# S4 plus eight experts on one core: S4 totals in one bf16 pass, weights' totals by DRAM, first block's transposed x kept, second block's operands stored in parts

## The chip, the core and the metric

The kernel runs on one core of a Trainium2 chip. The metric is the device time of the whole program in microseconds (us), lower is better. Times given are those of separate runs; the profile is of one further execution.

## The reference, cut to what matters

```python
xn = layernorm(u)                                   # 2048 tokens x 512
# S4: a convolution over the tokens, one kernel K for each of 512 channels
P = exp(logdA[:, :, None] * l); K = einsum("dn,dnl,dn->dl", Cc, P, dB).real
y = irfft(rfft(pad(xn.T)) * rfft(pad(K)))[:, :2048].T + xn * Dskip
# eight experts, all of them taken by every token (K = 8 of E = 8)
gates = softmax(xn @ w_gate)                        # sorted, then matched to e
for e in range(8):
    out += gates[:, e] * (silu(xn @ w1[e]) @ w2[e])   # w1 512x1792, w2 1792x512
return u + y + out
```

Inputs and results are float32.

## The kernel before

**Numbers in two halves.** TensorE works in float16. Every operand is split into a high and a low float16 half (`a = hi + lo`), and a product is three matmuls: hi·hi, hi·lo, lo·hi. So that the halves don't leave the range of float16, each operand is first scaled by a power of two that is worked out on the chip. For that a tile is squared with its row sums, the 128 row sums are added over the partitions, and the exponent of that *total* gives the scale. The addition over partitions is `pow2_total`: a float32 matmul with `ones` (128x128, float32) as weights and the row sums as a moving column; the result, in every partition, is copied out of PSUM by ACT. The tile is `tot_<name>`: `tot_k...` for the S4 kernels (32 of them), `tot_w...` for the experts' weights (two per expert, the first expert's w1 apart, 15 in all), `tot_a` and `tot_b` at the start.

**The experts.** Tokens are taken in NB = 4 blocks of 512, the hidden width 1792 in 7 pairs of 2x128, grouped as quads `d` = (0,1), (2,3), (4,5), (6). For each expert e, each block tb and each quad d, `block` makes the products of w1 in a Strassen-like form: seven products of combined operands (`xop`, seven combinations `o` of the four quarters of x, each in two halves `b`; `w1s`, seven combinations of w1), added in three PSUM tiles `hb` and partly in DRAM-accumulated SBUF tiles (`scC`, `scB` receive `sE` by an accumulating DMA of POOL's queue, L1493 `add`). ACT takes Silu from `hb` or `scC`/`scB` (L1324), writes the high half `ahl` (L1328), DVE the low half (L1337). `pop` then issues the second product with w2 (L1291 to L1293) into `y`, and `evacuate` scales it by the gate into `ye` (L1266) and adds it to `oacc` in DRAM through POOL (L1269). The products `product` (L1308) are matmuls of 128x256, the y matmuls 128x512. Expert 0's block 0 (`plain`, L1575) has no combined operands: it uses the transposed x of the first stage, `xT0`, and multiplies plainly.

**Slots.** The kernel is one long program with an order written out by hand. Each quad has four slots, each block sixteen; a slot is some 4.6 us of TensorE work. In `slot` the order is: functions of `mid`, then second products, low halves, functions of `side`, one or two steps of `work_on`, and then `bg_run`, the S4 work. `at(n, f)` puts f into slot n of expert 0; `early` and `copied` stand at other places of a slot. Every engine takes its queue in that order, so an instruction that waits holds up all behind it on its engine.

**Combined x.** For blocks 1 to 3 of expert 0, and again for block 0 (its combined operands are needed from expert 1 on), a stage in halves `(g, a)` works: `x_sums` (DVE), `x_high` (ACT), `x_low` (DVE), four `x_turn` (28 transposes in two matrices, L274, into the bank `s4`; ACT copies them into `xs`, L285, and SP stores them in `xd[g]`). Block 1's go straight to `xop`, and after the last one `xop` is stored whole in `xd[1]`: one DMA of 1.75 MB (L282). At each block's last quad `xop[:, o]` is loaded for the next block in seven parts.

**Weights.** While expert e−1 runs, the weights of expert e are read twice: `pp` tiles for the squares (`piece_square`), then `piece_end` (row sum, total, scales: three Items, each at least two slots after the other and only where the bank `s4` is free), then `raw` tiles for the split (`w1_split`, `w2_split`), which may begin once the third step is done.

**S4.** It is a generator whose DVE cost is paced: `bg_run` lets it run until its DVE estimate has used up `SHARE` × the TensorE time that has passed. Its matmuls (transforms `kf` L800, `uf` L787, `yp` L860, the kernels `kgen` L729, the totals) share one PSUM bank, tag "s4": `take_bank` gives it to a new user after the last one has been read, `bank_free` issues the pending read and says whether a new user may come. S4's result lands in `ys4`; in the last block `s4_final(i)` adds it to `oacc[i]` (POOL, L1477) and stores the output, one call at slot ⌊3i/4⌋. The last block's four tiles are loaded again by `final_load` and finished by DVE.

**SP's queue** carries all other loads and stores.

The lines that set the pace and the places of the moved work:

```python
own = SHARE * (clock["pe"] - clock["pe0"])
...
halves = [(g, a) for g in (2, 3, 0) for a in range(2)]
...
put((E - 1, NB - 1, i * 3 // 16, i * 3 // 4 % 4), lambda i=i: s4_final(i))
```

Of the kernel before, what the change touches and what calls it, by code (L numbers as in the profile page):

```python
# [8 lines left out]

F32 = mybir.dt.float32  # L10
F16 = mybir.dt.float16
I32 = mybir.dt.int32
AF = mybir.ActivationFunctionType
ALU = mybir.AluOpType
# [18 lines left out]
def s4_moe_kernel(  # L33
# [40 lines left out]

    ident = cp.tile([P, P], F16, name="ident")
    make_identity(nc, ident)
    ones = cp.tile([P, P], F32, name="ones")
    V.memset(ones, 1.0)
    halfpi = cp.tile([P, 1], F32, name="halfpi")
    V.memset(halfpi, math.pi / 2)  # L80
# [10 lines left out]
    oacc = [dr.tile([P, D], F32, name=f"oacc{i}") for i in range(NT)]  # L91
    ys4 = dr.tile([P, NT, D], F32, name="ys4")
    xnd = dr.tile([P, NT, D], F32, name="xnd")
    kds = [dr.tile([P, 4, 64], F32, name=f"kd{n}") for n in range(2)]


    uts = {}

    clock = {"slot": 0, "pe": 0.0, "pe0": 0.0, "dve": 0.0, "dve0": 0.0, "left": 0.0,
             "act": 0.0, "act0": 0.0, "pe1": 0.0, "actleft": 0.0}  # L100
    bank = {"out": None, "at": -1}

    def take_bank(out=None):
# [6 lines left out]

    def bank_free():

        if bank["out"]:
            take_bank()
        return clock["slot"] > bank["at"]

# [43 lines left out]

    def pow2_total(rows, n, nm, out=None):

        st = sb.tile([P, n], F32, tag="p2a", name=f"st_{nm}", bufs=2)
        def read():
            S.copy(st, tot[:, :n])
            if out:
                out()
        take_bank(read)
        tot = ps_s.tile([P, 512], F32, tag="s4", name=f"tot_{nm}")
        T.matmul(tot[:, :n], ones, rows, start=True, stop=True)  # L170
        return st

    def pow2_scale(dst, st, nm, add=0):
# [43 lines left out]
    xs_ = {}  # L217

    def x_stats(g):
        if g:  # L220
            xs_["rs8", g] = norm_stats(g)
        else:
            rs8 = xs_["rs8", 0] = sb.tile([P, TPB], F32, tag="rs8", name="rs8again")
            V.tensor_scalar(rs8, rstd[:, 0:TPB], float(2 ** XSH), None, op0=ALU.mult)

    def x_sums(g, a):

# [32 lines left out]
    def x_turn(g, a, q):  # L260


        hi, lo = xs_["hi"], xs_["lo"]
        if g == 1:
            parts = [(r // 4, r // 2 % 2, r % 2) for r in range(8 * q, min(8 * q + 8, 28))]
        else:
            b, o0 = q // 2, q % 2 * 4
            no = min(4, 7 - o0)
            parts = [(o0 + r // 2, b, r % 2) for r in range(2 * no)]
        n = len(parts)  # L270
        take_bank()
        tp = ps_s.tile([P, 8, P], F16, tag="s4", name=f"tp{g}_{a}_{q}")
        for r, (o, b, k) in enumerate(parts):
            T.transpose(tp[:, r, :], (hi, lo)[b][:, o, k * P:(k + 1) * P], ident)  # L274
        if g == 1:
            dst = xop.rearrange("p o a k t -> p (o a k) t")[:, 8 * q:8 * q + n, a * P:(a + 1) * P]
            if q % 2:
                V.tensor_copy(dst, tp[:, :n, :])
            else:
                S.copy(dst, tp[:, :n, :])  # L280
            if a and q == 3:
                nc.sync.dma_start(xd[1], xop)  # L282
        else:
            xs = sb.tile([P, 4, 2, P], F16, tag="hh", name=f"xs{g}_{a}_{q}", bufs=9)
            S.copy(xs.rearrange("p o k t -> p (o k) t")[:, :n], tp[:, :n, :])  # L285
            clock["act"] += at_(n * P)
            bank["at"] = now()
            for k in range(2):
                nc.sync.dma_start(xd[g][:, o0:o0 + no, b, k, a * P:(a + 1) * P], xs[:, :no, k])

    xp = {}

    def xplain(j, rs8):

        xn = sb.tile([P, D], F32, tag="fa", name=f"xn{j}")
# [161 lines left out]

    def w1_split(e, pr, raw):

        dst = w1s[pr].rearrange("p a o c -> p a (o c)")  # L460
        return hilo(dst[:, :, 0:6 * P], raw[:, 0:3, :].rearrange("p o c -> p (o c)"), w1_scale(e, pr))

# [2 lines left out]
        return hilo(dst[:, :, 6 * P:14 * P], tw.rearrange("p o c -> p (o c)"), w1_scale(e, pr))  # L465

    def w2_split(e, pr, raw):
        return hilo(w2s[pr].rearrange("p a f d -> p a (f d)"), raw.rearrange("p a c -> p (a c)"), scales[e][:, 1:2])

    class Item:  # L470
# [26 lines left out]
        return it  # L497

    def piece_end(e, w, n, ready):
        st = {}  # L500

        def s0(raw):
            st["g"] = prepass_end(e, w, n)
            step(0)
            clock["dve"] += 0.2

        def step(n):
            st["at"] = now()
            next(st["g"], None)
            done.add((e, w, n))  # L510

        def s1(raw):
            step(1)

        def s2(raw):
            step(2)
            clock["dve"] += 2.5
# [4 lines left out]
        for it in its:  # L522
            it.e, it.w = e, w
        return its

    def fetch():

# [344 lines left out]
    def at_(n):  # L872

        return n / 1050 + 0.17
# [10 lines left out]
    def now():  # L885
        return clock["slot"]
# [196 lines left out]
    def first_square(w, n, t, on_dve):  # L1083
# [2 lines left out]
        junk = tf  # L1086
        if w == 0:
            junk = w1s[n % 5 + 2][:, n // 5 % 2, 0:tf.shape[1] // TH, :].rearrange("p o c -> p (o c)")
            junk = junk.bitcast(mybir.dt.bfloat16)
# [93 lines left out]
    def plan(e):  # L1183
# [5 lines left out]
                work.append(piece_square(e, w, pr, at(1 + w)))  # L1189
            work.extend(piece_end(e, w, NPR, at(1 + w)))  # L1190
        def made(what, d):
            return lambda: (e - 1, NB - 1, what, d) in done and (e, "py".index(what), 2) in done
# [6 lines left out]
        yield from s4_all()  # L1199

    bg = background()
    SHARE = 0.90

    def bg_run():

# [217 lines left out]
    at(16, lambda: load_x(2))  # L1423
    at(42, s4_dft_load)
    at(19, lambda: x_sums(2, 0))
    halves = [(g, a) for g in (2, 3, 0) for a in range(2)]
    for n, (g, a) in enumerate(halves):
        s0 = 20 + 4 * n
        at(s0, lambda g=g, a=a: x_high(g, a), copied if n == 0 else side)
# [8 lines left out]
            turns.add(n1 - 2)  # L1438
        if a == 0:
            at(s0 + 3, lambda g=g: x_sums(g, 1))  # L1440
            if g:
                at(s0 + 3, lambda g=g: load_x((g + 1) % NB))
        elif g:
            if g + 1 < NB:
                at(s0 + 1, lambda g=g: norm_sums(g + 1))
            at(s0 + 2, lambda g=g: x_stats((g + 1) % NB))
            at(s0 + 3, lambda g=g: x_sums((g + 1) % NB, 0))

    def slot(e, tb, d, s, pops):
        for f in mid.get((e, tb, d, s), ()):  # L1450
# [215 lines left out]
```

## Time and profile before

| | |
|---|---|
| three runs | 2342.41, 2340.79, 2341.77 us; median 2341.77 |
| profiled execution | 2342.11 us, span 2340.3 us |
| granted TensorE clock, mean of the span | 0.998 |
| busy of the span | PE 99%, PEld 66%, DVE 84%, ACT 63%, POOL 15% |
| instructions | 45514 |
| DMA | 319.68 MB, mean 137 GB/s; 331079 packets |

PE is the matmul part of TensorE and PEld its weight loads, which overlap the matmuls; the printed lengths of matmuls overlap each other too, so what one costs is read from the distance between two starts. DVE is VectorE, ACT ScalarE, POOL GpSimd, SP the engine that issues most DMAs. A row of groups reads: line, engine, operation, output <- inputs, shape, count | busy us, mean ns of one | idle time just before, and what ended it. A row of the timeline reads: start, length, engine, line, operation, output <- inputs, shape, and in brackets the wait before it and its releaser.

### The profile page before, as it was taken

What the parts mean: (1) busy time and instruction counts of PE and PEld (TensorE: products, weight loads), DVE (VectorE), ACT (ScalarE), POOL (GpSimd) and SP (SyncE); (2) the same over time, 40 slices, a digit from 0 to 9 for tenths busy, and PEclk for the clock granted to TensorE, in tenths of its full rate; (3) what the DMA queues carried; (4) which work ended last, traced back from release to release, by engine and by line L of the source; (5) the groups of instructions that cost most, each with busy time, mean ns of one, the idle gap of its engine ahead of it and who ended that gap; (6) DMA issues with size and microseconds to landing.
All of it is one profiled execution on the core that took longest, in us unless ns stands there. A gap on an engine that the chain in (4) does not pass through costs nothing.

```text
span 2340.3 us, 45514 instructions
## 1 busy us (share of the span) xinstructions
PE 2323.6 (99%) x17818; PEld 1552.0 (66%) x17818; DVE 1965.9 (84%) x3821; ACT 1472.9 (63%) x2593; POOL 340.6 (15%) x394
## 2 busy tenths in 40 slices
PE   8999999999999999999999999999999999999999
PEld 4666666666666666666666666666666666666665
DVE  8864878889898899999999989999899988997721
ACT  7677667556666576665766657666566665764543
POOL 0001001121111211101111101111111110111112
PEclk9999999999999999999999999999999999999999
DMA  7586556674566655644556546565465653643456
GB/s 252 176 240 166 142 143 159 156 154 108 128 154 163 146 115 132 159 118 105 127 122 160 121 101 136 127 149 119 100 147 121 145 128 90 153 89 71 80 116 146
DMA packets 331079, 319.68 MB, mean 137 GB/s; under 512 B 190896, under 2 KB 224176, under 8 KB 330544
## 3 DMA queue, kind: packets, MB, share of 16 engines
q1 hardware_dynamic: 274416, 222.65, 32.6%
q0 software_dynamic: 55872, 93.61, 25.4%
q8 instruction: 139, 2.28, 0.4%
q14 instruction: 76, 0.62, 0.1%
q10 hardware_dynamic: 576, 0.52, 0.1%
HBM read 202.14 MB, written 65.01 MB: 114 GB/s over the span
## 4 chain that ended last, share of the span: by engine, by line
PE 93%; issue 2%; DMA 2%; ACT 2%; DVE 1%; POOL 0%; SPq 0%; DVEq 0%; POOLq 0%; ACTq 0%
PE hb L1308 41%; PE y L1293 15%; PE y L1292 15%; PE y L1291 15%; PE kgen L729 1%; PE kf L800 1%; PE yp L860 1%; PE uf L787 1%; DMA scB<-sE 1%; PE hb L1575 1%; DMA scC<-sE 0%; DMA oacc<-ye 0%; PE tp L274 0%; ACT ahl L1328 0%; ACT fa L1324 0%
## 5 line engine op out<-in xcount | busy, mean ns | idle before, releaser
L1308 PE MATMUL hb<-xop,w1s 128*128 128x256 f16 x9114 | 1072.9, 273 | 2.6 <-ACT scC L1522 2.4
L1308 PEld LDWEIGHTS <-w1s 128*128 128x128 f16 x9114 | 889.0, 98 | 171.2 <-issue 4.7
L1291 PE MATMUL y<-w2s,ahl 128*128 128x512 f16 x1792 | 679.2, 379 | 1.0 <-ACT ye L1266 1.0
L1293 PE MATMUL y<-w2s,ahl 128*128 128x512 f16 x1792 | 679.2, 379 | 0.0
L1292 PE MATMUL y<-w2s,ahl 128*128 128x512 f16 x1792 | 679.2, 379 | 0.0
L1293 PEld LDWEIGHTS <-ahl 128*128 128x128 f16 x1792 | 175.3, 98 | 211.4
L1493 POOL DMA_DIRECT2D scC<-sE x124 | 118.0, 951 | 1292.5 <-ACT sE L1522 1094.0
L1324 ACT ACTIVATE fa<-hb,sc 128x512 f32<-128x512 f32 (+1 forms) x252 | 160.5, 637 | 196.4 <-PE hb L1308 195.9
L1292 PEld LDWEIGHTS <-ahl 128*128 128x128 f16 x1792 | 175.3, 98 | 162.3 <-issue 1.3
L832 DVE TENSOR_TENSOR s<-s,tm 128x720 f32<-128x720 f32 (+14 forms) x480 | 268.9, 560 | 16.6
L1291 PEld LDWEIGHTS <-ahl 128*128 128x128 f16 x1792 | 175.3, 98 | 161.1
L831 DVE TENSOR_TENSOR tm<-v,k 128x720 f32<-128x720 f32 (+14 forms) x480 | 267.6, 557 | 10.3
L1337 DVE SCALAR_TENSOR_TENSOR ahl<-fa,sc,ahl 128x512 f16<-128x512 f32 (+1 forms) x262 | 178.8, 683 | 59.9 <-ACT ahl L1328 59.5
L1537 ACT COPY hb<-hb 128x512 f32<-128x512 f32 x124 | 64.2, 518 | 238.7 <-PE hb L1308 238.6
L1328 ACT ACTIVATE ahl<-fa,sc 128x512 f16<-128x512 f32 (+1 forms) x262 | 175.8, 671 | 8.5
L1527 ACT COPY hb<-hb 128x512 f32<-128x512 f32 x124 | 64.3, 519 | 175.2 <-PE hb L1308 174.3
L1493 POOL DMA_DIRECT2D scB<-sE x124 | 108.0, 871 | 424.1 <-ACT scB L1522 283.1
L1337 DVE SCALAR_TENSOR_TENSOR ahl<-scB,sc,ahl 128x512 f16<-128x512 f32 x124 | 84.5, 681 | 81.9 <-ACT ahl L1328 78.2
L717 DVE TENSOR_TENSOR tb<-ta,tt 128x64 f32<-128x64 f32 (+2 forms) x192 | 132.0, 688 | 5.7
L711 DVE TENSOR_TENSOR ta<-tb,zr 128x64 f32<-128x64 f32 (+2 forms) x192 | 131.7, 686 | 5.4
L1269 POOL DMA_DIRECT2D oacc<-ye x108 | 96.1, 1343 | 252.7 <-ACT ye L1266 251.1
L714 DVE TENSOR_TENSOR tt<-tb,zi 128x64 f32<-128x64 f32 (+2 forms) x192 | 130.5, 680 | 0.0
(245 smaller groups left out, 2444.2 us busy)
## 6 DMA issues: line engine op xcount, KB each, us to landing
xop<-xd SPq DMA_DIRECT2D x210, 256.0 KB, 4.0
pp<-in_w_dram SPq DMA_DIRECT2D x98, 512.0 KB, 4.2
raw<-in_w_dram SPq DMA_DIRECT2D x56, 512.0 KB, 4.7
oacc<-ye POOLq DMA_DIRECT2D x108, 256.0 KB, 6.3
scC<-sE POOLq DMA_DIRECT2D x93, 256.0 KB, 4.4
scB<-sE POOLq DMA_DIRECT2D x93, 256.0 KB, 4.0
raw<-in_w_dram SPq DMA_DIRECT2D x52, 256.0 KB, 3.8
raw<-in_w_dram SPq DMA_DIRECT2D x104, 128.0 KB, 3.7
```

Source lines behind the costliest of these rows:

```text
L711: V.tensor_tensor(ta, tin, zrv, op=ALU.mult)
L717: V.tensor_tensor(tout, ta, tt, op=ALU.add)
L831: V.tensor_tensor(tm, v3f[:, :, 0:n], kb, op=ALU.mult)
L832: V.tensor_tensor(s3[:, :, m:], s3[:, :, m:], tm, op=ALU.add)
L1291: T.matmul(y, lhs[0], w2s[pr][:, 0, fh, :], start=(c == 0), stop=False)
L1292: T.matmul(y, lhs[0], w2s[pr][:, 1, fh, :], start=False, stop=False)
L1293: T.matmul(y, lhs[1], w2s[pr][:, 0, fh, :], start=False, stop=(c == NF - 1))
L1308: T.matmul(dst[:, q, :], w1s[pr][:, a, wo, k * P:(k + 1) * P], xop[:, xo, b, k, :], start=(first_mm and q == 0 and n == 0), stop=(n == 5), ...
L1324: S.activation(fa, src[:, :n], AF.Silu, scale=w1_unscale(e, d if whole else prs[0]))
L1328: S.activation(ahl[:, 0, :n], fa, AF.Copy, scale=scales[e][:, 3:4])
L1337: V.scalar_tensor_tensor(ahl[:, 1, :n], fa, sc[:, 3:4], ahl[:, 0, :n], op0=ALU.mult, op1=ALU.subtract)
L1493: nc.gpsimd.dma_start(dst, src, accum_op=ALU.add)
```

## The change

Four parts, with some smaller ones.

- *Totals in one pass.* `ones` becomes bfloat16, and `pow2_total` reads the row sums as their upper 16 bits (`bitcast` to bfloat16, every second column). The scale depends on the exponent of the total. This holds for the 32 totals of S4, for `tot_a`, `tot_b` and expert 0's w2.
- *Weights' totals by DRAM.* For the experts from 1 on (14 totals) the matmul is replaced: row sum (DVE), `total_send` (SP stores 128 numbers), `total_fetch` (SP loads them into all partitions), an empty step, `total_sum` (ACT copies with a running sum), scales (DVE). `piece_end` is one Item of six steps, each at least two slots after the last. It asks no longer for the bank.
- *First block's x kept.* `xT0` is sent to DRAM (`x0_send`: normalized x in four stores, three of its quarters' pairs straight into `xd[0]` in six, the whole as `x0d`) in slots 2 to 11, loaded again (`x0_load`), and the four other combinations are made from it by DVE and ACT (`x0_sums`, `x0_high`, `x0_low`, slots 35 to 40), already transposed. The stage's halves (0, 0) and (0, 1) with their transposes go.
- *Block 1's operands in parts.* `xd[1]` is stored in seven DMAs of 256 KB, one a slot from slot 20 on, in place of the one after the last `x_turn`.
- *Smaller.* `SHARE` 0.905; the calls of `s4_final` regrouped in the first slots of each half quad; `clock["two"]` keeps the reads of the bank out of the second step of a slot with two steps of weight work; the first stage's `xn` tiles lie in the ring "hh".

```diff
-    ones = cp.tile([P, P], F32, name="ones")
+    ones = cp.tile([P, P], BF16, name="ones")
...
         if bank["out"]:
+            if clock["two"]:
+                return False
             take_bank()
...
+        high = rows.bitcast(BF16)[:, 1::2]
...
-        T.matmul(tot[:, :n], ones, rows, start=True, stop=True)
+        T.matmul(tot[:, :n], ones, high, start=True, stop=True)
...
+    def total_send(row, nm):
+        rd = dr.tile([P, 1], F32, name=f"rd_{nm}")
+        nc.sync.dma_start(rd, row)
+        return rd
+    def total_fetch(rd, nm):
+        bt = sb.tile([P, P], F32, tag="bt", name=f"bt_{nm}", bufs=1)
+        nc.sync.dma_start(bt, rd.rearrange("p a -> (p a)").partition_broadcast(P))
+        return bt
+    def total_sum(bt, nm):
+        st = sb.tile([P, 1], F32, tag="p2a", name=f"st_{nm}", bufs=2)
+        S.activation(bt, bt, AF.Copy, accum_out=st)
+        clock["act"] += at_(P) + 0.2
         return st
...
-            if a and q == 3:
-                nc.sync.dma_start(xd[1], xop)
...
+    def x0_send(n):
+        if n < 4:
+            nc.sync.dma_start(xnd[:, n, :], xp["xn", n])
+        elif n < 7:
+            k, t = ((0, 0), (2, 0), (2, TH))[n - 4]
+            for b in range(2):
+                nc.sync.dma_start(xd[0][:, n - 4, b], xT0[:, b, k:k + 2, t:t + TH])
+        else:
+            nc.sync.dma_start(x0d, xT0)
+    def x0_load():
+        xs_["x0"] = sb.tile([P, 2, KT, TB], F16, tag="tb", name="x0", bufs=1)
+        nc.sync.dma_start(xs_["x0"], x0d)
+    def x0_sums(k):
+        x0 = xs_["x0"]
...
+        V.tensor_tensor(r.rearrange("p h a t -> p h (a t)"), x0[:, 0, k::2, :], x0[:, 1, k::2, :], op=ALU.add)
+        V.tensor_tensor(s, r[:, 0, 1, :], r[:, 1, 1, :], op=ALU.add)
+        V.tensor_tensor(f[:, 0, :], s, r[:, 0, 0, :], op=ALU.subtract)
+        V.tensor_tensor(f[:, 1, :], r[:, 0, 1, :], r[:, 0, 0, :], op=ALU.subtract)
+        V.tensor_tensor(f[:, 2, :], r[:, 1, 0, :], f[:, 0, :], op=ALU.subtract)
+    def x0_high(k):                       # two ACT copies into hi
...
+    def x0_low(k):                        # two DVE subtractions into lo
...
+        for b, x in enumerate((hi, lo)):
+            nc.sync.dma_start(xd[0][:, 3:7, b, k, :], x)
...
-        st = pow2_total(r, 1, f"w{e}_{w}")
-        yield
-        if bank["out"]:
-            take_bank()
+        if e:
+            rd = total_send(r, f"w{e}_{w}")
+            yield
+            bt = total_fetch(rd, f"w{e}_{w}")
+            yield
+            yield
+            st = total_sum(bt, f"w{e}_{w}")
+            yield
+        else:
...
     def piece_end(e, w, n, ready):
...
-        def later():
-            return now() > st["at"] + 1 and bank_free() and now() + 1 not in turns
-        its = [Item(None, [s0], ready), Item(None, [s1], later), Item(None, [s2], later)]
+        it = Item(None, [lambda raw, k=k: step(k) for k in range(6)],
+                  lambda: now() > st["at"] + 1 if "at" in st else ready())
...
+        clock["two"], n2 = False, limit
...
+            clock["two"] = limit == 0 and n2 == 2
...
-    SHARE = 0.90
+    SHARE = 0.905
...
-    halves = [(g, a) for g in (2, 3, 0) for a in range(2)]
+    halves = [(g, a) for g in (2, 3) for a in range(2)]
...
+    for o in range(7):
+        at(20 + o, lambda o=o: nc.sync.dma_start(xd[1][:, o], xop[:, o]))
+    for n in range(4):
+        at(2 + n // 2, lambda n=n: x0_send(n))
+        at(8 + n, lambda n=n: x0_send(4 + n))
+    for k in range(2):
+        at(35 + 3 * k, lambda k=k: x0_sums(k))
+        at(36 + 3 * k, lambda k=k: x0_high(k))
+        at(37 + 3 * k, lambda k=k: x0_low(k))
...
-        put((E - 1, NB - 1, i * 3 // 16, i * 3 // 4 % 4), lambda i=i: s4_final(i))
+        n = (i + 2) // 3
+        put((E - 1, NB - 1, n // 2, n % 2 * 3), lambda i=i: s4_final(i))
```

More of the change, by code (lines that the diff above doesn't have):

```diff
@@ L11 @@
 F16 = mybir.dt.float16
+BF16 = mybir.dt.bfloat16
 I32 = mybir.dt.int32
@@ L93, in s4_moe_kernel @@
     xnd = dr.tile([P, NT, D], F32, name="xnd")
+    x0d = dr.tile([P, 2, KT, TB], F16, name="x0d")
     kds = [dr.tile([P, 4, 64], F32, name=f"kd{n}") for n in range(2)]
@@ L99, in s4_moe_kernel @@
     clock = {"slot": 0, "pe": 0.0, "pe0": 0.0, "dve": 0.0, "dve0": 0.0, "left": 0.0,
-             "act": 0.0, "act0": 0.0, "pe1": 0.0, "actleft": 0.0}
+             "act": 0.0, "act0": 0.0, "pe1": 0.0, "actleft": 0.0, "two": False}
     bank = {"out": None, "at": -1}
@@ L169, in pow2_total @@
         tot = ps_s.tile([P, 512], F32, tag="s4", name=f"tot_{nm}")
-        T.matmul(tot[:, :n], ones, rows, start=True, stop=True)
+        T.matmul(tot[:, :n], ones, high, start=True, stop=True)
+        return st
+    def total_send(row, nm):
[10 more added lines that the diff above has]
+        clock["act"] += at_(P) + 0.2
         return st
@@ L219, in x_stats @@
     def x_stats(g):
[L220 to L224, printed above, removed]
+        xs_["rs8", g] = norm_stats(g)
     def x_sums(g, a):
@@ L289, in x_turn @@
                 nc.sync.dma_start(xd[g][:, o0:o0 + no, b, k, a * P:(a + 1) * P], xs[:, :no, k])
+    def x0_send(n):
[12 more added lines that the diff above has]
+        x0 = xs_["x0"]
+        r = sb.tile([P, 2, 2, TH], F32, tag="k4", name=f"x0r{k}", bufs=1)
+        f = xs_["f0"] = sb.tile([P, 3, TH], F32, tag="v3", name=f"x0f{k}", bufs=1)
+        s = xs_["s0"] = sb.tile([P, TH], F32, tag="z", name=f"x0s{k}", bufs=1)
+        V.tensor_tensor(r.rearrange("p h a t -> p h (a t)"), x0[:, 0, k::2, :], x0[:, 1, k::2, :], op=ALU.add)
[4 more added lines that the diff above has]
+    def x0_high(k):
+        hi = xs_["hi"] = sb.tile([P, 4, TH], F16, tag="ta", name=f"x0h{k}", bufs=1)
+        S.copy(hi[:, 0], xs_["s0"])
+        S.copy(hi[:, 1:4].rearrange("p o t -> p (o t)"), xs_["f0"].rearrange("p o t -> p (o t)"))
+        clock["act"] += at_(4 * TH)
+    def x0_low(k):
+        hi = xs_["hi"]
+        lo = sb.tile([P, 4, TH], F16, tag="tt", name=f"x0l{k}", bufs=1)
+        V.tensor_tensor(lo[:, 0], xs_["s0"], hi[:, 0], op=ALU.subtract)
+        V.tensor_tensor(lo[:, 1:4].rearrange("p o t -> p (o t)"), xs_["f0"].rearrange("p o t -> p (o t)"),
+                        hi[:, 1:4].rearrange("p o t -> p (o t)"), op=ALU.subtract)
+        for b, x in enumerate((hi, lo)):
+            nc.sync.dma_start(xd[0][:, 3:7, b, k, :], x)
     xp = {}
     def xplain(j, rs8):
-        xn = sb.tile([P, D], F32, tag="fa", name=f"xn{j}")
+        xn = xp["xn", j] = sb.tile([P, D], F32, tag="hh", name=f"xn{j}", bufs=9)
         V.tensor_scalar(xn, uts[0][j], mean[:, j:j + 1], rs8[:, j:j + 1], op0=ALU.subtract, op1=ALU.mult)
@@ L407, in prepass_end @@
         yield
-        st = pow2_total(r, 1, f"w{e}_{w}")
-        yield
-        if bank["out"]:
-            take_bank()
+        if e:
[7 more added lines that the diff above has]
+        else:
+            st = pow2_total(r, 1, f"w{e}_{w}")
+            yield
+            if bank["out"]:
+                take_bank()
         if w == 0:
@@ L458, in w1_split @@
     def w1_split(e, pr, raw):
+        assert e == 0 or (e, 0, 5) in done
         dst = w1s[pr].rearrange("p a o c -> p a (o c)")
@@ L467, in w2_split @@
     def w2_split(e, pr, raw):
+        assert e == 0 or (e, 1, 5) in done
         return hilo(w2s[pr].rearrange("p a f d -> p a (f d)"), raw.rearrange("p a c -> p (a c)"), scales[e][:, 1:2])
@@ L499, in piece_end, with step @@
     def piece_end(e, w, n, ready):
[L500 to L507, printed above, removed]
+        st = {"g": prepass_end(e, w, n)}
+        def step(k):
             st["at"] = now()
             next(st["g"], None)
[L510 to L517, printed above, removed]
-        def later():
-            return now() > st["at"] + 1 and bank_free() and now() + 1 not in turns
-        its = [Item(None, [s0], ready), Item(None, [s1], later), Item(None, [s2], later)]
-        for it in its:
-            it.e, it.w = e, w
-        return its
+            done.add((e, w, k))
+            clock["dve"] += (0.2, 0.0, 0.0, 0.0, 0.0, 0.9)[k]
+        it = Item(None, [lambda raw, k=k: step(k) for k in range(6)],
+                  lambda: now() > st["at"] + 1 if "at" in st else ready())
+        it.e, it.w = e, w
+        return [it]
     def fetch():
@@ L1088, in first_square @@
             junk = w1s[n % 5 + 2][:, n // 5 % 2, 0:tf.shape[1] // TH, :].rearrange("p o c -> p (o c)")
-            junk = junk.bitcast(mybir.dt.bfloat16)
+            junk = junk.bitcast(BF16)
         r = rows_of(0, w)[:, n:n + 1]
@@ L1191, in made @@
         def made(what, d):
-            return lambda: (e - 1, NB - 1, what, d) in done and (e, "py".index(what), 2) in done
+            return lambda: (e - 1, NB - 1, what, d) in done and (e, "py".index(what), 5) in done
         a = [piece_w1(e, pr, made("p", d)) for d, prs in enumerate(DQS) for pr in prs]
@@ L1440, in s4_moe_kernel @@
             at(s0 + 3, lambda g=g: x_sums(g, 1))
[L1441 to L1447, printed above, removed]
+            at(s0 + 3, lambda g=g: load_x(g + 1) if g + 1 < NB else x0_load())
+        elif g + 1 < NB:
+            at(s0 + 1, lambda g=g: norm_sums(g + 1))
+            at(s0 + 2, lambda g=g: x_stats(g + 1))
+            at(s0 + 3, lambda g=g: x_sums(g + 1, 0))
+    for o in range(7):
[7 more added lines that the diff above has]
+        at(37 + 3 * k, lambda k=k: x0_low(k))
     def slot(e, tb, d, s, pops):
```

## The prediction

> **What bounds the kernel now.** I read the page's busy line and its chain first, then the waits, then single stretches of the timeline.
>
> ```profile
> PE 2323.6 (99%) x17818; PEld 1552.0 (66%) x17818; DVE 1965.9 (84%) x3821; ACT 1472.9 (63%) x2593; POOL 340.6 (15%) x394
> PE 93%; issue 2%; DMA 2%; ACT 2%; DVE 1%; POOL 0%; SPq 0%; DVEq 0%; POOLq 0%; ACTq 0%
> PE hb L1308 <- ACT scC L1522: 2.4, 4, 0.9
> ```
>
> TensorE is the end-setting engine for 93% of the chain, and its largest listed wait in the whole span is 2.4 us. So a matmul that goes away is worth its issue interval, and little else is to be had. An issue interval is read from the starts in the timeline (the printed lengths overlap):
>
> ```profile
> 328.23 0.28 PE L170 MATMUL tot_k<-krow,ones 128*128 128x1 f32 x2
> 328.37 0.81 PE L1308 MATMUL hb<-xop,w1s 128*128 128x256 f16 x6
> 201.54 0.24 PE L353 MATMUL lg<-wgs,xop 128*128 128x8 f16 x4
> 201.64 2.12 PE L1308 MATMUL hb<-xop,w1s 128*128 128x256 f16 x18
> 112.76 0.61 PE L274 MATMUL tp<-ident,xh 128*128 128x128 f16 x8
> 113.20 0.38 PE L1291 MATMUL y<-w2s,ahl 128*128 128x512 f16 x1
> ```
>
> One f32 total (two records) holds TensorE 328.37 − 328.23 = 0.14 us. Four narrow f16 matmuls, each with its own weight load, hold it 0.10, so 0.025 each. Eight transposes hold it 0.44, so 0.055 each.
>
> The second resource is VectorE: in the middle of the S4 work it is nearly full (columns: PE, PEld, DVE, ACT, POOL busy).
>
> ```profile
> 1114.00:1186.00 72.00, 72.00 (x552) 48.40 (x551) 68.14 (x121) 48.13 (x80) 10.48 (x12) 1.00 0.56 133
> ```
>
> **The change, part by part.** How often each thing runs:
>
> ```profile
> L170 PE MATMUL tot_k<-krow,ones x64: 167/208/250, 328.2 to 2169.6; 128*128 128x1 f32 x64
> L170 PE MATMUL tot_w<-r,ones x30: 167/208/250, 33.5 to 1951.5; 128*128 128x1 f32 x30
> L274 PE MATMUL tp<-ident,xh x112: 219/219/219, 62.2 to 215.7; 128*128 128x128 f16 x112
> L274 PE MATMUL tp<-ident,xl x112: 219/219/219, 62.3 to 222.4; 128*128 128x128 f16 x112
> ```
>
> Two records are one total: 32 S4 totals and 15 weights' totals. The first expert's total stays on TensorE, the other 14 leave it: 14 × 0.14 = 1.96 us. The 32 S4 totals become one bf16 matmul of one column. No row has a bf16 matmul; the nearest is the narrow f16 one with 0.025, so 32 × (0.14 − 0.025) = 3.68 us. Bounds: half the f32 time would leave 2.24, nothing at all would give 4.48, and an unchanged price would give 0. The Trainium skill, page "TensorE: Matmul & The Clock Gate", section "Weight-path perf modes", has the short weight load for 128 columns of any type but FP32, so for bf16 too; here f16 loads stand at 98 ns and no run before the change shows bf16.
>
> The 224 transposes are eight half blocks of 28. The first block's two halves go, as its transposed x of the first stage is kept: 56 × 0.055 = 3.08 us. With them go eight ACT copies and four ACT casts; two smaller additions, casts and subtractions per half take their place on ACT and DVE, which have more room before S4 starts than later.
>
> At the start three more totals become single passes. The first is on the way to the first long matmul.
>
> ```profile
> 12.75 0.53 PE L170 MATMUL tot_a<-row,ones 128*128 128x1 f32 x2
> 13.14 1.01 PE L308 MATMUL tp<-ident,xhl 128*128 128x128 f16 x8
> ```
>
> It holds TensorE 0.39 us, the two others 0.14 or a little more. A single pass each saves 0.1 to 0.6 together; I take 0.4. TensorE's sum is 1.96 + 3.68 + 3.08 + 0.4 = 9.1 us.
>
> **The second block's operands in parts.** Before, a single store of 1.75 MB goes out just ahead of the first accumulating add.
>
> ```profile
> 96.63 0.33 SPq L282 DMA_DIRECT2D xd<-xop  x1
> 96.82 1.03 POOL L1493 DMA_DIRECT2D scC<-sE  x1 [95.51 <-DVE xop L278]
> 106.74 0.72 ACT L1324 ACTIVATE scC<-scC,sA 128x512 f32<-128x512 f32 x1 [2.84 <-DMA scC<-sE]
> 108.84 0.38 PE L1291 MATMUL y<-w2s,ahl 128*128 128x512 f16 x1 [1.01 <-ACT ye L1266]
> 115.31 1.36 PE L1308 MATMUL hb<-xop,w1s 128*128 128x256 f16 x11 [0.65 <-ACT scC L1522]
> ```
>
> The add needs 9.9 us to land, ACT stands 2.84 us for it, is late with the ye copies, and TensorE idles 1.01 and then 0.65 us. After the change seven stores of 256 KB leave from slot 20 on; the instruction order puts the first behind the ye copies, so nothing large is ahead of this add. ACT then comes out of its casts without that wait, by more than TensorE idled: −1.7 us. What is late next is nothing within 1 us, since 2.84 exceeds 1.7. The seven stores pass scC and scB adds, the xs stores and the pp loads between 109 and 143 us:
>
> ```profile
> xd<-xop SPq DMA_DIRECT2D x1, 1792.0 KB, 6.5
> oacc<-ye SPq DMA_DIRECT2D x4, 256.0 KB, 2.1
> ```
>
> By the second row seven pieces take 7 × 2.1 = 14.7 us of landings spread over some 34 us, against 6.5 in one lump; I put 0 on TensorE for it, bounds 0 to 1.7.
>
> The Trainium skill, page "DMA: Bandwidth & Descriptors", section "Measured (HBM→SBUF, 128 partitions, SWDGE, issued from GpSimd)", says the reverse: batch transfers to 1 MiB and more. By its fit (2.0 us and 436 KB a us), an estimate, seven pieces take 18 us against 6; the row of 9.9 us shows why the lump may yet be the dearer one here.
>
> **The weights' totals by DRAM.** Each is now six steps, at least two slots apart: DVE row sum, SP store of 128 numbers, SP load spread to all partitions, nothing, ACT sum, DVE scales. On SP the load waits for the store's landing, and what is queued behind it are weight loads and xop loads. The same round trip exists for S4's kernel:
>
> ```profile
> SPq L745 <- DMA kd<-ksb: 103.9, 32, 8.7
> DMA to landing us min/median/max: 1.6/1.8/5.9
> ```
>
> (The second row is that of tile kt, the load back.) A store takes 103.9/32 = 3.2 us of SP's waiting, where the load follows at once. In the new order the load stands 4 to 14 us of TensorE work behind its store, and the ACT sum at least 13 behind the load; the trip is covered by that spacing and costs 0, with 8.7 and 5.9 as worst cases. ACT gains 14 sums with an accumulator read, under 14 × (0.37 + 0.19) us by these rows, less 14 small copies:
>
> ```profile
> L738 ACT COPY ksb<-kgen 128x256 f32<-128x256 f32 x32 | 11.9, 372 | 1.0
> L438 ACT ACTIVATION_READ_ACCUMULATOR pp<-pp 128x1 f32 x98 | 19.0, 194 | 0.0
> L285 ACT COPY xs<-tp 128x1024 f16<-128x1024 f16 (+1 forms) x24 | 21.7, 902 | 2.3 <-PE tp L274 2.3
> ```
>
> The eight xs copies that go (8 × 0.9 = 7.2) about pay for it. The scales come some 5 to 20 us later after the row sum than before, but the first weight split of an expert moves by +1 to −14 us in the order, so no product waits.
>
> **The tail.** The last sums into oacc move in POOL's and SP's queues.
>
> ```profile
> 2290.27 0.84 POOL L1477 DMA_DIRECT2D oacc<-ys  x1 [3.39 <-DMA oacc<-ye]
> 2292.75 0.82 POOL L1477 DMA_DIRECT2D oacc<-ys  x1 [1.64 <-DMA oacc<-ye]
> 2302.76 0.72 ACT L1324 ACTIVATE scB<-scB,sc 128x512 f32<-128x512 f32 x1 [3.95 <-DMA scB<-sE]
> 2316.16 0.72 ACT L1324 ACTIVATE scB<-scB,sc 128x512 f32<-128x512 f32 x1 [1.44 <-DMA scB<-sE]
> 2317.95 1.25 PE L1308 MATMUL hb<-xop,w1s 128*128 128x256 f16 x10 [0.66 <-ACT scC L1522]
> ```
>
> POOL stood 5.0 us for the ye sums, with the scB add behind it. In the new order that add precedes the two waiting sums, so it leaves about 4.5 us sooner, more than ACT's 3.95; and no sum into oacc comes just ahead of the next scB add. I take −0.7 for the 0.66. Against it, three sums now go out together after that add, ahead of the last scC add; that one's result is used in the last 3 us, over 10 us later: 0, bound +1.
>
> **What comes back.** SHARE rises from 0.90 to 0.905, and S4 moves by up to 30 us against the expert work. Where ACT has S4's kernel copies in front of scC, TensorE waits:
>
> ```profile
> 367.00 0.37 ACT L738 COPY ksb<-kgen 128x256 f32<-128x256 f32 x1
> 367.70 0.71 PE L1308 MATMUL hb<-xop,w1s 128*128 128x256 f16 x5 [0.92 <-ACT scC L1522]
> ```
>
> In the new order this meeting is gone at that place, but the same one (split, two kernel copies, scC) appears in expert 3's first block, and three sine calls stand before hb's copy in expert 6. DVE work per TensorE time rises by about 0.5%, 68.14 to 68.5 of 72, so it keeps up on average; in expert 3's last block the order bunches some 21 DVE instructions in a slot, which the 8 us between a hidden tile and its use should cover. I take +0.5 us, bounds −1.1 and +3.
>
> **The sum.** −9.1 − 1.7 − 0.7 + 0.5 = −11.0 us. The profiled execution took 2342.11 us (span 2340.3 and 1.8 around it), 0.34 above the median of the three runs, 2341.77. So the profiled one becomes 2331.1 and the median 2330.8.
>
> **Rivals.** (1) ACT and DVE give the time back: with PE faster and S4 denser, five more waits of 0.92 us: 2330.8 + 4.6 = 2335.4. For it: DVE's 68.14 of 72; against: only 2.4 us of such waits in all of before. Chance 0.17. (2) The pieces crowd the adds: two waits of ACT like the 2.84, each returned as 1.7 us on TensorE, 2330.8 + 3.4 = 2334.2. This is where the DMA page's rule would show. Chance 0.08. (3) It doesn't do what it says: a bf16 total holds TensorE as long as the f32 one, 2330.8 + 3.68 + 0.4 = 2334.9. Chance 0.05. (4) Slower: the totals' round trip is late. ACT takes its queue in order, so the sum waits for the broadcast with hb's copies behind it. It decides once a broadcast lands later than 13 us after its place. If each of 14 costs what the scC wait cost (2.84 on ACT, 1.7 on TensorE), 14 × 1.7 = 23.8: 2354.6. Against: 8.7 and 5.9 are the longest of that kind. Chance 0.05. The forecast has 0.65.
>
> **Range and chances.** Low end: all unknowns good (S4 totals 0.8 more, tail and start 0.5, ACT waits −1.6), 2330.8 − 2.9 = 2327.9. High end: half-price totals (+1.4), no start gain (+0.4), the block-1 and tail waits still there (+2.4), new waits +2.5: 2337.5. That takes in rivals 1 to 3. About 0.2%, 4.7 us, is what a measurement here can tell from no change, so the line is at 2337.1: faster 0.88 (forecast and nearly all of 1 to 3), same 0.07, slower 0.05.
>
> **What would show it.** Right: 32 bf16 records for tot_k, about 0.025 us from one start to the next; no tp rows after the third block's; no ACT wait for scC near 104 us; no tot_w beyond the first; TensorE's idle before scB and scC in the last 40 us gone. Wrong: ACT rows of the totals' sum with a DMA wait in front, more and longer "PE hb" waits on ACT in the list, DVE windows above 70 of 72, or tot_k at 0.1 us and more.

## The result, and the profile after

The changed kernel takes 2331.97 us in the median of six runs (2330.66 to 2333.64), the kernel before 2342.17 (2340.79 to 2343.15). The ratio is 0.9958, 95% interval 0.9945 to 0.9970. A second set of runs gave 2331.63 against 2341.62, ratio 0.9957 [0.9943, 0.9971]. The profiled execution took 2332.46 us with a span of 2330.7, 9.65 less than before; 11.0 were forecast.

The page of the changed kernel, busy line and chain:

```profile
PE 2314.2 (99%) x17699; PEld 1538.6 (66%) x17699; DVE 1963.8 (84%) x3816; ACT 1467.0 (63%) x2599; POOL 339.9 (15%) x394
PE 97%; DMA 1%; ACT 1%; DVE 0%; issue 0%; SPq 0%; DVEq 0%; ACTq 0%
```

TensorE has 119 records fewer and still sets the end. The waits of the changed kernel, those of TensorE's products alone (total, times, longest):

```profile
PE hb L1372 <- DMA xop<-xd: 2.3, 2, 1.5
PE hb L1372 <- ACT scC L1594: 0.7, 3, 0.3
```

The first row is new: no product waited for an `xop` load before. The second was 2.4 us.

The timeline of the changed kernel at one S4 total, TensorE only:

```profile
322.52 0.17 PE L178 MATMUL tot_k<-krow,ones 128*128 128x1 bf16 x1
322.55 1.69 PE L1372 MATMUL hb<-xop,w1s 128*128 128x256 f16 x14
```

From start to start the bf16 total holds TensorE 0.03 us, in the median of 32 it is 0.028; the float32 one held it 0.14. The tile tp of the changed kernel:

```profile
L297 PE MATMUL tp<-ident,xh x84: 219/219/219, 61.7 to 172.8; 128*128 128x128 f16 x84
L297 PE MATMUL tp<-ident,xl x84: 219/219/219, 61.8 to 180.1; 128*128 128x128 f16 x84
```

168 transposes in place of 224. ACT's timeline of the changed kernel where it stood 2.84 us for the first scC add:

```profile
102.65 0.83 ACT L273 CAST xh<-xfb 128x768 f16<-128x768 f32 x1
103.39 0.72 ACT L1388 ACTIVATE scC<-scC,sA 128x512 f32<-128x512 f32 x1
104.14 0.72 ACT L1392 ACTIVATE ahl<-scC,sc 128x512 f16<-128x512 f32 x1
104.77 1.25 ACT L1330 ACTIVATE ye<-y,gse 128x512 f32<-128x512 f32 x2
```

No bracket: nothing is waited for. The add itself lands in 3.4 us in place of 9.9, by the DMA view of the changed kernel from 95 to 97 us:

```profile
scC<-sE POOLq DMA_DIRECT2D x1, 256.0 KB, 3.4
```

For the whole I took, for every two neighbouring matmuls, the distance of their starts less the median for that pair of lines, and summed what exceeds 0.035 us after 100 us (without 32 equal steps of 0.05 us inside the `kgen` matmuls, which both kernels have). These standing times are 5.1 us before and 4.5 after. So the work itself became 9.65 − 0.56 = 9.1 us shorter (9.1 forecast); 0.4 of it lies ahead of the first product with w2, where executions of the same code differ by 1 us. The waits only changed places: 1.98 went at block 1 and 1.10 in the tail, but 1.65 came at 514.6 and 1.01 at 1376.5. The timeline there, changed kernel, TensorE:

```profile
514.62 1.42 PEld L1372 LDWEIGHTS <-w1s 128*128 128x128 f16 x14 [1.97 <-DMA xop<-xd]
514.63 1.59 PE L1372 MATMUL hb<-xop,w1s 128*128 128x256 f16 x13 [1.48 <-DMA xop<-xd]
```

And SP's queue ahead of it, same kernel:

```profile
504.01 0.42 SPq L184 DMA_DIRECT2D rd_w<-r  x1
504.52 1.81 SPq L1590 DMA_DIRECT2D xop<-xd  x4
512.77 0.32 SPq L190 DMA_DIRECT2D bt_w<-rd_w  x1
513.18 1.34 SPq L1590 DMA_DIRECT2D xop<-xd  x2
```

The load that TensorE waits for left at 504.52, ahead of the waiting load back (512.77). So it isn't SP's standing that made it late. It was long under way. The DMA view of the changed kernel from 504 to 513 (KB each, us to landing):

```profile
xop<-xd SPq DMA_DIRECT2D x4, 256.0 KB, 10.5
scC<-sE POOLq DMA_DIRECT2D x1, 128.0 KB, 11.8
rd_w<-r SPq DMA_DIRECT2D x1, 0.5 KB, 8.7
```

These transfers beside the store of 128 numbers take 10 us and more, on POOL's queue too; an xop load's median over the whole span is 4.1. The windows view says the same: in the changed kernel

```profile
506.00:513.00 7.00, 7.00 (x43) 3.87 (x40) 6.76 (x13) 2.21 (x5) 3.20 (x4) 1.00 0.86 50
```

the DMA engines count as 86% busy (last but one column) while 50 GB/s move (last column). And the stores themselves, the line L184 of the changed kernel:

```profile
DMA to landing us min/median/max: 7.4/8.6/12.8
```

All 14 are slow, for 0.5 KB. My forecast had 8.7 us as a worst case and nothing for the neighbours.

### The profile page after: what moved, and what is told of

Same layout as the page of the kernel before. It is cut to its first block, busy times and chain, and to the rows that moved or that the text cites. A ratio compares the mean times of both kernels' runs of the same rounds, so it can differ in the third digit from the quotient of the medians.

```text
span 2330.7 us, 45267 instructions
## 1 busy us (share of the span) xinstructions
PE 2314.2 (99%) x17699; PEld 1538.6 (66%) x17699; DVE 1963.8 (84%) x3816; ACT 1467.0 (63%) x2599; POOL 339.9 (15%) x394
## 4 chain that ended last, share of the span: by engine, by line
PE 97%; DMA 1%; ACT 1%; DVE 0%; issue 0%; SPq 0%; DVEq 0%; ACTq 0%
PE hb L1372 42%; PE y L1357 16%; PE y L1356 16%; PE y L1355 16%; PE hb L1647 2%; PE kgen L793 1%; DMA xop<-xd 1%; PE uf L851 1%; PE yp L924 1%; PE kf L864 1%; PE tp L297 0%; ACT ahl L1392 0%; ACT ye L1330 0%; DMA ut0b<-in_u_dram 0%; ACT scB L1388 0%
## 5 line engine op out<-in xcount | busy, mean ns | idle before, releaser
L1401 DVE SCALAR_TENSOR_TENSOR ahl<-scC,sc,ahl 128x512 f16<-128x512 f32 x124 | 84.3, 680 | 70.1 <-ACT ahl L1392 69.9
```

What stands on the lines that cost most here:

```text
L1401: V.scalar_tensor_tensor(ahl[:, 1, :n], fa, sc[:, 3:4], ahl[:, 0, :n], op0=ALU.mult, op1=ALU.subtract)
```

## The experiments

### The weights' totals: where the late loads come from

Four kernels on one chip.

> The changed kernel once more, for the same chip as the three beside it: 2332.0 us, 2330.5 to 2333.7 by its first six runs. In its first profile TensorE stood 1.65 us at 514.6 and 1.01 us at 1376.5 for xop loads that landed 10.1 and 11.0 us after their issue (median 4.1). Whether these two stand there again in a second profile tells if they belong to the kernel or to that execution: both theories below say they do.

Measured: 2331.63 (2330.66 to 2332.79). The wait at 514.5 stands again, 1.25 us; the one at 1376 does not. So the first belongs to the kernel, the size of either to the execution. The first also stands, with 0.32 to 1.49 us, in the four runs below that keep the DRAM trip (fetch_later, f32_totals, share_090, final_before).

> Changed kernel, but the weights' totals of experts 1 to 7 are back on TensorE, as single bf16 passes; no stores of 128 numbers, no loads back. TensorE issues 14 more matmuls of 0.028 us: +0.39. Theory (the store of 128 numbers of 4 bytes holds up all transfers near it, and the late xop loads come from that): the two waits go, -2.66, so 2331.97 - 2.66 + 0.39 = 2329.7, and no xop load takes over 9 us. Rival (the loads are late because S4's own transfers in packets of 64 bytes now meet them): 2331.97 + 0.39 = 2332.4, xop loads of 10 us and more remain. Rival of the prediction (the trip is covered and costs nothing): 2332.4 as well.

```diff
-        if e:
-            rd = total_send(r, f"w{e}_{w}")
...
-        else:
-            st = pow2_total(r, 1, f"w{e}_{w}")
+        st = pow2_total(r, 1, f"w{e}_{w}")
...
-        it = Item(None, [lambda raw, k=k: step(k) for k in range(6)], ...)
+        def later():
+            return now() > st["at"] + 1 and bank_free() and now() + 1 not in turns
+        its = [Item(None, [lambda raw, k=k: step(k)], later if k else ready) for k in (0, 1, 5)]
```

Measured: 2329.77 (2329.39 to 2330.73), ratio to the kernel before 0.9948 [0.9936, 0.9961]. That is 1.9 us less than the changed kernel beside it, though TensorE has 14 matmuls more. The waits for xop loads are gone, the longest such load takes 7.7 us, and the standing times are 1.13 us in all. The same seven microseconds in the windows view, and 504 to 513 in the DMA view of this kernel:

```profile
506.00:513.00 7.00, 7.00 (x46) 4.27 (x45) 6.79 (x13) 2.55 (x6) 3.55 (x4) 1.00 1.06 259
```

```profile
xop<-xd SPq DMA_DIRECT2D x6, 256.0 KB, 5.6
scC<-sE POOLq DMA_DIRECT2D x1, 128.0 KB, 5.9
```

259 GB/s in place of 50, with S4's small packets still there. The theory's number (2329.7) came out; the two rivals at 2332.4 did not.

> Changed kernel, but the empty step of the six stands between the store and the load back, not behind the load: the load comes at least four slots after its store, so SP's queue should not stand for it (28.2 us of SP's waits in 6 places before, under 5 expected). Theory (the store holds up transfers, SP's standing costs nothing): same time as the changed kernel within 0.7 us, 2331.3 to 2332.7, xop loads of 10 us remain. Rival (SP's standing delays the xop loads behind it): the 2.66 us go, 2329.3.

```diff
             rd = total_send(r, f"w{e}_{w}")
             yield
+            yield
             bt = total_fetch(rd, f"w{e}_{w}")
             yield
-            yield
```

Measured: 2331.42 (2330.93 to 2332.06). SP's waits of this kernel, the load back:

```profile
SPq L190 <- DMA rd_w<-r: 5.8, 1, 5.8
```

It was 28.2 us in 6 places in the changed kernel. SP's standing is gone, the time is the same, and a wait of 1.4 us for an xop load stands at 516.2. So SP's standing cost nothing.

> As w_totals_tensor, and beside each of the 14 totals SP stores the 128 row sums in a place of DRAM that nobody reads: 128 packets of 4 bytes into 512 bytes in a row. Nothing waits for these stores. Theory (the store itself holds up transfers): the stores land after 7 to 13 us, packets of 2 KB of 2 to 7 us stand behind them, and 1 to 3 us come back: 2330.7 to 2332.7. Rival (S4's transfers): as w_totals_tensor within 0.5 us. Rival (SP standing at the load back): as w_totals_tensor, since no load waits.

```diff
         st = pow2_total(r, 1, f"w{e}_{w}")
+        if e:
+            sd = dr.tile([P, 1], F32, name=f"sd_{e}_{w}")
+            nc.sync.dma_start(sd[:, 0:1], r)
```

Measured: 2336.10 (2334.52 to 2337.16), 6.3 us more than without the stray stores: the right way, and two to six times the size I had expected. Nothing reads these stores. The waits and ACT's timeline of this kernel:

```profile
PE tot_k L178 <- ACT k L864: 3.0, 1, 3.0
```

```profile
795.42 0.72 ACT L1385 ACTIVATE scB<-scB,sc 128x512 f32<-128x512 f32 x1 [4.26 <-DMA scB<-sE]
796.80 0.57 ACT L864 COPY k<-kf 128x512 f32<-128x512 f32 x1
```

A held-up scB add kept ACT 4.26 us, with S4's copy behind it and TensorE behind that. And then, windows view of this kernel (the third figure from the end is the granted clock):

```profile
794.00:797.40 3.40, 0.39 (x2) 0.10 (x1) 0.55 (x2) 1.95 (x4) 0.00 (x0) 1.00 1.10 264
797.60:801.30 3.70, 3.61 (x16) 2.19 (x16) 3.67 (x5) 2.25 (x7) 1.06 (x2) 0.54 0.87 242
801.30:805.00 3.70, 3.70 (x25) 2.27 (x24) 3.60 (x8) 1.47 (x3) 2.46 (x3) 1.00 0.93 170
```

TensorE stood for some 3.4 us and was then granted 0.54 of its clock for 3.7 us. By the starts the idle cost 3.4 and the slow stretch another 1.6; a second wait, 1.4 us at 1593.9, makes up the rest. The waits of 1.2 to 1.7 us in the other kernels left the clock at 1.00. The Trainium skill, page "TensorE: Matmul & The Clock Gate", section "Why this matters for your kernels", asks for no idle gap of TensorE over about 3 us; this trace agrees.

Then the place that the 128 numbers go to:

> As stray_row, but the 128 numbers go to places 512 bytes apart: the same 128 packets of 4 bytes, no two in one row of 512 bytes. stray_row was 6.3 us slower than w_totals_tensor, its stores landed after 8.2 to 11.6 us, in nine places stood packets of 2 KB of 3 to 7 us behind them. Theory (the writes queue up because they fall in one small place of the memory): stores land in 2 to 4 us, no such packets, time as w_totals_tensor, 2329.8. Rival (128 packets of 4 bytes are dear wherever they go): landing 8 us and more, 2334 to 2337.

> As stray_row and stray_wide, but the 128 numbers go to places 64 bytes apart, eight of them in each 512 bytes. With 4 bytes apart the stores landed in 8.2 to 11.6 us and the kernel was 6.3 us slower than without them; with 512 bytes apart they landed in 1.5 to 4.3 us and it cost nothing. Theory A (writes queue up only where they share one piece of 64 bytes or less): landing 1.5 to 4.3 us, 2329.8. Theory B (they queue up within 512 bytes, eight at a time, in 16 places side by side): landing little longer, under 5 us, 2329.8 to 2330.5. Theory C (they queue up over the whole 8 KB): 8 us and more, 2334 to 2337.

```diff
-            sd = dr.tile([P, 1], F32, name=f"sd_{e}_{w}")     # stray_row
+            sd = dr.tile([P, P], F32, name=f"sd_{e}_{w}")     # stray_wide; [P, 16] in stray_64
```

Measured: stray_wide 2329.75 (2329.27 to 2331.28), stray_64 2330.28 (2330.12 to 2331.08), against 2329.77 without stores (these two ran on another chip; the kernel before takes 2341.57 and 2341.55 on it, and 2341.62 on the first). The landing of the 14 stores in stray_row, stray_wide and stray_64, from the tile view of each:

```profile
DMA to landing us min/median/max: 8.2/8.9/11.6
```

```profile
DMA to landing us min/median/max: 1.5/3.5/4.3
```

```profile
DMA to landing us min/median/max: 1.5/3.6/4.8
```

The same 128 packets of 4 bytes are dear when they lie side by side in 512 bytes, and cheap at 64 and at 512 bytes apart. Theory C falls; A and B aren't told apart by landings of 3.5 and 3.6 us and ranges that overlap. The single packets in the traces show the neighbours too. After 150 us, packets of 2 KB that take over 3 us are 55 in the changed kernel and 53 in stray_row, each time in seven places; there is none in the kernel before, in w_totals_tensor, in stray_wide and in stray_64. The 4-byte packets of a store take 0.01 us each and have started within 3 us of its issue, packed (changed kernel at 504.0, stray_row at 781.9) or spread (stray_64 at 782.2); what is long is the time from there to the landing. What the memory does in that time isn't seen in any trace; 8.6 us for 128 would fit one after another at 0.07 us each, but that is arithmetic, not shown.

### The other parts

> Changed kernel with float32 ones and the whole row sums again: 32 S4 totals, the first expert's w2 total and the two at the start are two-pass once more. By the starts in the two profiles a total is 0.140 us in float32 and 0.028 in bf16: 33 x 0.112 = 3.7, and 0.4 at the start, so 2331.8 + 4.1 = 2335.9. Rival (the bf16 total is not cheaper on the path, the gain came from elsewhere): 2331.8. With float32 totals the S4 work is placed the same but for fractions of a microsecond, so the late xop loads near 510 stay.

```diff
-    ones = cp.tile([P, P], BF16, name="ones")
+    ones = cp.tile([P, P], F32, name="ones")
...
-        high = rows.bitcast(BF16)[:, 1::2]
...
-        T.matmul(tot[:, :n], ones, high, start=True, stop=True)
+        T.matmul(tot[:, :n], ones, rows, start=True, stop=True)
```

Measured: 2334.58 (2333.64 to 2335.35), 2.9 more than the changed kernel, 4.1 expected. Along its trace it falls back by 0.112 us at each total, as it should. But its wait for the late load near 515 is 0.32 us, against 1.25 in the second profile of the changed kernel; that accounts for 0.9 of the missing 1.2.

> Kernel before with one part alone: xd[1] stored in seven DMAs of 256 KB from slot 20 on. The waits at 108.84 (1.17) and 115.31 (0.81) go: -1.98, so 2341.8 - 2.0 = 2339.8. Rival (the pieces crowd the accumulating adds, one wait of ACT returned as 1.7 us): 2341.5. Rival (the lump was not what delayed the add, something else in that stretch was): 2341.8 with both waits still there.

Measured: 2339.66 (2338.88 to 2340.87), 1.9 less than the kernel before, with 2.0 expected; ratio 0.9992 [0.9983, 1.0000]. Both waits are gone from its trace. In the changed kernel's DMA view from 105 to 150 us the pieces stand so:

```profile
xd<-xop SPq DMA_DIRECT2D x7, 256.0 KB, 4.1
```

7 × 4.1 = 29 us of landings against 6.5 for the lump, twice what I had put, but no product waits for any of them. The Trainium skill, page "DMA: Bandwidth & Descriptors", section "Measured (HBM→SBUF, 128 partitions, SWDGE, issued from GpSimd)", says to batch transfers to 1 MiB and more; by the sum of the landings these rows agree. The edit changes size and moment together: no run stores the lump whole at a later slot, so which of the two frees the add is open.

> Kernel before with one part alone: the first block's transposed x kept in DRAM, its 56 transposes, eight xs copies and the second normalization gone. 56 x 0.055 = 3.08 us: 2341.8 - 3.1 = 2338.7. The waits at 108.8 and 115.3 (2.0 us) stay. Rival (the six stores of quarters, x0d and its load crowd other transfers, or the new DVE sums in slots 35 to 40 give waits): 2340 to 2342.

> x0_only once more with SHARE at 0.905 in place of 0.90, as the changed kernel has it. x0_only was 20.4 us slower than the kernel before; its trace has TensorE standing 18.6 us at 2269.8 for the last S4 transform, whose input DVE finished late, and running at a granted clock of 0.50 until 2274. Up to 2000 us it was 2 to 3 us ahead. In the new order of instructions the last S4 transform stands at product 13938 of 14490 as in the kernel before, not at 13956 with nothing left to hide it. Theory (the part itself brings 3.1, and S4, paced too low, came to its deadline late): the wait goes, 2341.7 - 3.1 = 2338.6. Rival (keeping x in DRAM is dear by itself): above 2345.

x0_only takes over the diff's lines on `x0d`, `x0_send` to `x0_low`, `xp["xn", j]` and `halves`; x0_only_905 adds `SHARE = 0.905`.

Measured: x0_only 2361.95 (2361.11 to 2364.05), ratio 1.0085 [1.0071, 1.0099], a bad miss; x0_only_905 2339.83 (2339.02 to 2340.99), ratio 0.9992 [0.9983, 1.0001]. The waits of x0_only and its windows:

```profile
PE yp L904 <- ACT ysb L911: 18.6, 1, 18.6
```

```profile
2251.00:2269.70 18.70, 0.21 (x1) 0.00 (x0) 16.96 (x33) 0.98 (x2) 0.73 (x1) 0.57 0.11 30
2269.70:2274.00 4.30, 4.23 (x20) 2.85 (x20) 0.77 (x2) 0.01 (x1) 0.00 (x0) 0.50 0.29 34
```

DVE alone is at work (16.96 of 18.70): S4 must be done before the last block, and wasn't. S4's matmuls stand up to 330 products (some 50 us) later than in the kernel before, at the same SHARE. With 0.905 S4 ends where it ended before, and 22 us are gone. The part itself shows between the products 600 and 1200 of both traces (those with `xop` and with w2 counted), where 56 transposes go: x0_only_905 gains 3.11 us there, as worked out. By the medians only 1.7 is left. In the profile S4's other places cost 1.1 (3.1 us of waits outside block 1 and the tail, 2.0 before), and the first product with w2 starts 0.8 later; the latter is no sign of the part, as parts_only, whose code is unchanged up to there, starts it 1.0 later.

> Changed kernel with SHARE at 0.90. In its order the last S4 transform stands at product 13956, the deadline, some 18 products of TensorE work (3 us) closer behind the one before it than S4's pace asks; in x0_only it was short by some 198 and TensorE stood 18.6 us. Theory (DVE is short in proportion): a wait of 1 to 3 us at the deadline, 2332.8 to 2334.8. Rival (DVE has that much room, no wait): 2331.8. Rival (S4 falls over the edge as in x0_only): 2350.

Measured: 2334.86 (2333.73 to 2337.42), 3.2 more. The size is at the upper end of the theory's, and the cause is another: the trace has no wait at the deadline. ACT's timeline of share_090 shows what it has instead:

```profile
863.20 1.13 ACT L515 ACTIVATE w1s<-tw,sc 128x1024 f16<-128x1024 f32 x1
864.24 1.13 ACT L515 ACTIVATE w2s<-raw,sc 128x1024 f16<-128x1024 f32 x1
865.28 0.36 ACT L1609 COPY hb<-hb 128x256 f32<-128x256 f32 x1
```

Two splits in a row stand ahead of the copy of hb, and TensorE waits 0.80 us at 865.7 and 0.79 at 869.1. S4's places decide which weight step falls where. So with all parts together a SHARE of 0.90 costs 3.2 us but doesn't miss the deadline, as it did in x0_only. One difference, which stands in the code and not in the list of the change, gives S4 room there: the last step of a weights' total counts 0.9 us of DVE in the pacing in place of 2.5, over 14 totals 22 us. That this is what saves share_090 is not shown; no run takes it back alone. Which of its executions reach 2337.4, and why, is open.

> Changed kernel with the calls of s4_final at the slots of the kernel before. The two waits of TensorE in the last 40 us of the kernel before, 0.28 and 0.82 us behind ACT's waits for the scB adds, are gone in the changed kernel's trace; they come back: 2331.8 + 1.1 = 2332.9. Rival (the order of the final sums plays no part, the adds landed sooner by chance): 2331.8.

```diff
-        n = (i + 2) // 3
-        put((E - 1, NB - 1, n // 2, n % 2 * 3), lambda i=i: s4_final(i))
+        put((E - 1, NB - 1, i * 3 // 16, i * 3 // 4 % 4), lambda i=i: s4_final(i))
```

Measured: 2331.73 (2329.82 to 2332.94), the same as the changed kernel. POOL's timeline and ACT's wait in the tail of this kernel:

```profile
2282.25 0.84 POOL L1548 DMA_DIRECT2D oacc<-ys  x1 [3.39 <-DMA oacc<-ye]
2283.75 0.82 POOL L1548 DMA_DIRECT2D oacc<-ys  x1 [0.66 <-DMA oacc<-ye]
2284.28 1.20 POOL L1564 DMA_DIRECT2D scB<-sE  x1
```

```profile
2292.69 0.72 ACT L1388 ACTIVATE scB<-scB,sc 128x512 f32<-128x512 f32 x1 [1.90 <-DMA scB<-sE]
```

POOL stands 4.05 us here (5.03 before), the scB add is held up as before, ACT waits 1.90 (3.95 before), and TensorE doesn't wait at all. Nor does it in the tail of parts_only, which has the old order too. In the changed kernel ACT has no wait for this add. So the new order does free ACT, but TensorE's two waits of 0.28 and 0.82 us are gone without it as well. Since parts_only has the tail's order of the kernel before and no such wait, they seem to belong to the one execution profiled there; a second profile of that kernel, which would show it, isn't on record.

## Why the prediction was right

Time, sign and range came out, partly by luck: a cost that the prediction put at nothing stood against gains that came out larger than forecast. By its own steps:

- *What bounds the kernel:* right. But 2.4 us isn't the largest wait listed in the span; among TensorE's waits before there is a longer one, at the start. No term rests on it.

```profile
PE tp L308 <- ACT xhl L298: 6.9, 1, 6.9
```

- *Totals in one pass:* right. 0.028 us against the 0.025 that I took from a narrow f16 matmul; 32 × 0.112 = 3.58 in place of 3.68.
- *Transposes:* right. Between the products 600 and 1200 the changed kernel gains 3.39 us; 56 × 0.055, one total of 0.14 and a wait of 0.10 that went make 3.3. With the part nearly alone (x0_only_905) it is 3.11.
- *Start, 0.4:* not to be told apart. The first product with w2 (`y`) starts at 41.44 us before, at 41.02 and 41.30 in two profiles of the changed kernel, and at 42.44 in parts_only, which has the code of the kernel before up to there.
- *Block 1's operands, −1.7:* right, −1.98 by the trace and −1.9 by the part alone. The pieces' landing was set too short (2.1, measured 4.1), without effect.
- *The totals by DRAM, "covered, costs 0":* this step failed. The trip was covered, each ACT sum starts 5 us or more after its numbers have landed. But I costed only who waits for the trip, and not what the trip does to transfers beside it. It cost 2.66 us of waits in one profile and 1.25 in the next, and 1.9 us net against totals in one pass on TensorE. The fourth rival had the trip late in ACT's queue; there was no such wait.
- *Tail, −0.7:* near in number (−1.10) by luck: the order frees ACT as forecast, but TensorE's waits are gone with the old order too.
- *What comes back, +0.5:* the waits that are neither in block 1, nor in the tail, nor for xop loads sum to 1.9 us after and 2.0 before, so nothing; the meetings moved (290.1, 578.8, 905.8, 1556.8) and were no more than before. Counted with the late loads, which it didn't have in mind, the term is +2.5, inside its bounds of −1.1 and +3. That SHARE's rise also gains something, and isn't only a risk, I had not seen: without it the whole change is 3.2 us slower, and the x0 part alone falls off S4's deadline.

So, in the two profiles, the work gave −9.1 (9.1 forecast), block 1 −2.0, the tail −1.1 and the rest +2.5, together −9.65 in place of −11.0: the late loads took 2.0 us more than the term had, block 1 and the tail gave 0.7 more.

The best version is w_totals_tensor: the change with its weights' totals on TensorE, 2329.77 us.

## What to carry to other kernels

When something is moved off a full engine to a queue, cost what it does to its neighbours there, not only its own latency: here 1.96 us of matmul time was bought with late loads, and once the operation had become cheap (0.14 to 0.028 us) moving it was no longer worth anything. Where background work has a deadline, look how near to it the old order stood before a part is judged alone. And a wait that one profile shows is not yet a wait of the kernel: see whether a relative with the same order shows it too.

## What the runs showed of the hardware

- A store of one float per partition into 512 bytes of DRAM in a row landed after 7.4 to 12.8 us. In the changed kernel the xop loads issued up to 6 us after it took 9.7 us in the median and the scC and scB adds of POOL's queue 8.2 and 8.8; those issued elsewhere took about 4. With the numbers 64 or 512 bytes apart it landed in 1.5 to 4.8 us, and the same loads and adds beside it took 3.0 to 3.4.
- TensorE idle for 3.4 us was followed by 3.7 us at a granted clock of 0.54, and idle for 18.7 us by 0.50 for over 4 us; after 1.7 us the clock stayed at 1.00.
- A matmul of one column in bf16, 128 deep, held TensorE 0.028 us, in float32 0.140.
